# When the q and k of late attention steps are prepared: a reordering between VectorE, ScalarE and the pieces of an MLP

## Chip, core, metric

One core of a Trainium2 chip (trn2). The time is device microseconds of one execution, the median of several. All executions quoted were fast, with a granted TensorE clock of 0.997 to 1.0. A profile is one execution; its span (202.6 us before) is some 1.75 us shorter than its device time (204.35 us in that execution).

Names: PE is TensorE, DVE is VectorE, ACT is ScalarE, POOL is GpSimd, SPq is the queue of DMA issues of SyncE. A "piece" is about 0.87 us of MLP matmuls that the program can place freely; `fill(n)` emits n of them. In the lines of the profile, gT is the gelu output of the first MLP layer, gs the sums of its blocks, MA to MD the PSUM banks of the second layer's products, qkT the transposed q and k, and Hps, S, OK, O and K the banks of the first layer and of attention.

## The reference, cut

```python
# attention in blocks of 64, B=4, H=8, S=768, D=64, with a decay lam per head
intra = (qb @ kb^T) * Dmask ;  out = intra @ vb + (qb * lam_pow) @ kv_state
kv_state = lam**64 * kv_state + (kb * rev_pow)^T @ vb
# then an MLP over x = out as [3072, 512]
g = gelu_tanh(x @ w_in)        # 512 -> 2048
return g @ w_out               # 2048 -> 512
```

## The kernel before

Attention runs in 24 steps (a batch, 256 tokens, half the heads). For each step q, k and v are loaded, prepared (scaled and cast to 16 bits) and q and k transposed; the MLP of finished groups fills PE between the steps. The second MLP layer forms two-by-two block products from sums of blocks (`gs`), so VectorE works for PE before and after each product.

```python
qkp = ctx.enter_context(tc.tile_pool(name="qkp", bufs=4))      # transposed q and k
ps_M = ctx.enter_context(tc.tile_pool(name="psM", bufs=8, space=PSUM))  # all PSUM banks

def prep_qk(s):
    ...
    q_eng = nc.gpsimd if s == 3 else nc.vector
    pin(q_eng.tensor_tensor(wide(tq), q32[:], decay(dq, s), ALU.mult))       # L243
    ...
    pin(nc.scalar.activation(out=wide(tk), in_=k32[:], func=AF.Copy))        # L248
    ...
    if s >= FIRST_DMA_T:                                                     # 9
        pin(nc.sync.dma_start_transpose(out=o..., in_=tqk...))               # L252
# prep_v: v scaled on GpSimd (L230), then the load of step s + 3 is issued

def sum_g(i0, i1, ms=None):        # the sums gs of the second layer, on VectorE
    ...
    pin(nc.vector.tensor_tensor(gsum[m][:, i, :], block(...), block(...), op))   # L531

def product(m, p):                 # one piece: 8 matmuls, banks MA, MB, MC, MD
    ...
    elif m == 6:                   # after the last product of a pair
        pin(tt(d, banks["D"][:], d, ALU.add))                                # L587
```

The order of the late steps, which the change touches:

```python
for n in range(8, 16):
    stage_t(n)
    prep_qk(n + 2) if n == 8 else prep(n + 2)
    fill(3 if n == 14 else 2)
    R(n, n - 1)                    # scores of n, values of n - 1
    ...
for n in range(16, NSTEP + 1, 2):
    if n + 2 < NSTEP:
        prep(n + 2)
    fill(2)
    burst((n, n + 1) if n < NSTEP else (), (15,) if n == 16 else (n - 2, n - 1))
    if n == NSTEP:
        break
    fill(2)
    U(n)
    U(n + 1)
    if n + 3 < NSTEP:
        prep(n + 3)
    fill(14 if n % 4 else 8)
```

`burst` is the attention stretch of two steps: scores S (L295), values O (L379), states K (L393). Every L before belongs to this file.

## Time and profile before

| | before |
|---|---|
| time, 3 runs | 203.91 us (203.87 to 204.37) |
| span of the profile | 202.6 us |
| PE busy | 194.3 us, 96% |
| VectorE busy | 145.4 us, 72% |

PE is the bound: from 17 us to 199 us its matmuls follow each other, but for a few holes. An instruction of PE that starts later than the one before it allows is the thing to look for, not the idle share of other engines.

### The profile page before, as it was taken

To read this page: it belongs to the slowest core of one execution; us is meant where nothing else is said; L and a number is where in the kernel's file an instruction comes from. 1 tells how busy PE (TensorE), PEld (TensorE's weight loads), DVE (VectorE), ACT (ScalarE), POOL (GpSimd) and SP (SyncE) were. 2 spreads that over 40 slices of the span, in tenths; PEclk is the share of its full clock that TensorE was granted. 3 is DMA by queue.
4 is the path that set the end of the run, shared out by engine and by line. 5 is a ranking of instruction groups with operands and counts; after the bars stand their busy time and mean duration, and the time that the engine had idled before them with its cause. 6 is when DMAs were issued, how large, how long until landed. Compare 5 with 4: busy or idle time off the path is not lost.

```text
span 202.6 us, 5666 instructions
## 1 busy us (share of the span) xinstructions
PE 194.3 (96%) x2348; PEld 129.9 (64%) x2348; DVE 145.4 (72%) x293; ACT 107.8 (53%) x205; POOL 66.3 (33%) x80
## 2 busy tenths in 40 slices
PE   6789999999999999999999999999999999999993
PEld 1456544456888888654688764688664688545882
DVE  5896623889999989968799749889556471334753
ACT  2465778375993473487642378524367414466210
POOL 6594132457358254162541609203402000000000
PEclk9999999999999999999999999999999999999999
DMA  6999999999999999999975999305510003300014
GB/s 173 290 328 389 383 387 377 289 292 308 345 256 220 266 207 240 204 271 166 239 193 115 282 230 208 70 0 130 133 58 3 0 0 107 104 0 0 3 45 162
DMA packets 64202, 37.85 MB, mean 187 GB/s; under 512 B 17585, under 2 KB 59569, under 8 KB 64177
## 3 DMA queue, kind: packets, MB, share of 16 engines
q1 hardware_dynamic: 63344, 36.97, 72.1%
q10 hardware_dynamic: 832, 0.52, 0.8%
q8 instruction: 18, 0.29, 0.6%
q14 instruction: 8, 0.06, 0.1%
HBM read 27.26 MB, written 6.29 MB: 166 GB/s over the span
## 4 chain that ended last, share of the span: by engine, by line
PE 77%; DVE 11%; SPq 4%; DMA 4%; issue 2%; ACT 1%; DVEq 0%
PE Hps L484 34%; PE MD L555 7%; PE MB L555 7%; PE O2ps L499 7%; PE MA L555 7%; DVE gs L531 4%; SPq L70 4%; DMA wi<-in_moe_w_in_dram 4%; PE MC L555 3%; PE Hps L601 3%; PE S L295 2%; DVE qk L243 2%; DVE PT L305 2%; PE OK L353 1%; PE Tps L266 1%
## 5 line engine op out<-in xcount | busy, mean ns | idle before, releaser
L484 PE MATMUL Hps<-xT,w_in 128*128 128x512 f16 (+1 forms) x416 | 78.7, 346 | 0.0
L488 ACT ACTIVATE gT<-Hps 128x512 f16<-128x512 f32 x88 | 52.3, 597 | 29.5 <-PE Hps L484 28.5
L484 PEld LDWEIGHTS <-w_in 128*128 128x128 f16 x416 | 40.3, 98 | 33.7
L531 DVE TENSOR_TENSOR gs<-gT 128x1024 f16<-128x1024 f16 (+1 forms) x62 | 39.9, 699 | 18.5 <-ACT gT L488 18.5
L456 POOL TENSOR_TENSOR u<-t,lumask 128x256 f16<-128x256 f32 x40 | 29.4, 747 | 67.8 <-DVE t L449 49.8
L555 PEld LDWEIGHTS <-gs 128*128 128x128 f16 x400 | 38.9, 98 | 5.0 <-DVE gs L531 0.5
L305 DVE TENSOR_TENSOR PT<-S,mask 128x512 f16<-128x512 f32 x48 | 30.4, 681 | 9.5 <-PE S L295 9.5
L230 POOL TENSOR_TENSOR v<-v,dv 128x512 f16<-128x512 f32 x24 | 28.5, 1193 | 4.9 <-PE S L295 1.7
L555 PE MATMUL MA<-w_sum,gT 128*128 128x256 f16 x160 | 19.5, 273 | 0.4 <-DVE o L587 0.3
L555 PE MATMUL MB<-w_out,gs 128*128 128x256 f16 x160 | 19.1, 273 | 0.0
L555 PE MATMUL MD<-w_sum,gs 128*128 128x256 f16 x152 | 18.6, 273 | 0.3 <-DVE gs L531 0.3
L562 ACT ACTIVATE m<-MB 128x512 f32<-128x512 f32 x10 | 6.0, 597 | 23.9 <-PE MB L555 23.9
L248 ACT ACTIVATE qk<-k 128x512 f16<-128x512 f32 x24 | 15.0, 626 | 6.8 <-DMA k<-in_k_dram 6.8
L243 DVE TENSOR_TENSOR qk<-q,dq 128x512 f16<-128x512 f32 x23 | 18.5, 803 | 0.0
L555 PEld LDWEIGHTS <-gT 128*128 128x128 f16 x160 | 15.4, 98 | 3.5 <-ACT gT L488 0.5
L430 ACT ACTIVATE xT<-OK 128x256 f16<-128x256 f32 x29 | 11.2, 455 | 8.0 <-PE OK L353 7.7
L499 PE MATMUL O2ps<-w_out,gT 128*128 128x512 f16 x64 | 14.6, 379 | 0.0
L566 DVE TENSOR_TENSOR o<-MA,m 128x512 f32<-128x512 f32 x10 | 6.9, 688 | 10.2 <-ACT m L562 10.2
L128 DVE TENSOR_TENSOR w_sum<-w_out 128x1024 f16<-128x1024 f16 x10 | 8.9, 932 | 6.4 <-POOL w_out L118 3.5
L430 ACT ACTIVATE xT<-O 128x256 f16<-128x256 f32 x18 | 6.4, 458 | 10.2 <-PE O L404 7.9
L295 PEld LDWEIGHTS <-qkT 64*64 64x64 f16 x384 | 6.0, 106 | 7.0 <-issue 3.2
L449 DVE SCALAR_TENSOR_TENSOR t<-t,lamu,OK 128x64 f32<-128x64 f32 x44 | 10.1, 273 | 0.5
(68 smaller groups left out, 168.7 us busy)
## 6 DMA issues: line engine op xcount, KB each, us to landing
q<-in_q_dram SPq DMA_DIRECT2D x24, 256.0 KB, 5.2
k<-in_k_dram SPq DMA_DIRECT2D x24, 256.0 KB, 5.2
v<-in_v_dram SPq DMA_DIRECT2D x23, 256.0 KB, 5.3
out_dram<-o SPq DMA_DIRECT2D x22, 256.0 KB, 4.5
wo<-in_moe_w_out_dram SPq DMA_DIRECT2D x4, 1024.0 KB, 9.5
wi<-in_moe_w_in_dram SPq DMA_DIRECT2D x4, 512.0 KB, 7.8
wi<-in_moe_w_in_dram SPq DMA_DIRECT2D x2, 1024.0 KB, 12.8
v<-in_v_dram ACTq DMA_DIRECT2D x1, 256.0 KB, 4.3
```

The source lines that it names most:

```text
L230: pin(nc.gpsimd.tensor_tensor(wide(tv[:]), ld32[s][2][:], decay(dv, s), ALU.mult))
L243: pin(q_eng.tensor_tensor(wide(tq), q32[:], decay(dq, s), ALU.mult))
L248: pin(nc.scalar.activation(out=wide(tk), in_=k32[:], func=AF.Copy))
L305: pin(nc.vector.tensor_tensor(t[:, hl].rearrange("p b c d -> p b (c d)"), Sps[:].rearrange("p b c d -> p b (c d)"), mask[:].unsqueeze(1).t ...
L430: pin(nc.scalar.activation(out=d, in_=o, func=AF.Copy))
L449: pin(nc.vector.scalar_tensor_tensor(t[:, hp, :], state[half][:, hp, :], lamu[:, 2 * half + hp : 2 * half + hp + 1], K[:, hp, :], ALU.mult ...
L456: pin(nc.gpsimd.tensor_tensor(u[:], state[half][:].unsqueeze(2).to_broadcast([P, 2, 2, D]), lumask[:, 2 * half : 2 * half + 2, :].unsqueez ...
L484: pin(nc.tensor.matmul(by_block(Hps[:, i, :]), w_in16[:, c, f * P : (f + 1) * P], x(c), start=(c == 0), stop=(c == NC - 1)))
L488: pin(nc.scalar.activation(out=dst, in_=Hps[:], func=AF.Gelu_apprx_tanh))
L499: pin(nc.tensor.matmul(O2[tau][0][:], gT[:, f % HF, f // HF, tau * P : (tau + 1) * P], w_out16[:, f, :], start=(n == 0), stop=(n == NF - 1)))
L531: pin(nc.vector.tensor_tensor(gsum[m][:, i, :], block(T0, F0, i), block(T1, F1, i), op))
L555: pin(nc.tensor.matmul(dst, lhsT, rhs, start=(i == 0), stop=(i == HF - 1), skip_group_check=True))
```

## The change

Intent: have q and k of late steps ready earlier than two pieces ahead of the attention stretch that they are prepared before, and keep the preparation of step 11 from standing in front of the MLP's work.

```diff
     for n in range(8, 16):
         stage_t(n)
+        fill(1 if n == 9 else 0)
         prep_qk(n + 2) if n == 8 else prep(n + 2)
-        fill(3 if n == 14 else 2)
+        fill({9: 1, 14: 3}.get(n, 2))
         R(n, n - 1)
...
-    for n in range(16, NSTEP + 1, 2):
-        if n + 2 < NSTEP:
-            prep(n + 2)
-        fill(2)
-        burst((n, n + 1) if n < NSTEP else (), (15,) if n == 16 else (n - 2, n - 1))
-        if n == NSTEP:
-            break
+    prep(18)
+    fill(2)
+    for n in range(16, NSTEP, 2):
+        burst((n, n + 1), (15,) if n == 16 else (n - 2, n - 1))
         fill(2)
         U(n)
         U(n + 1)
-        if n + 3 < NSTEP:
-            prep(n + 3)
-        fill(14 if n % 4 else 8)
+        for m in (n + 3, n + 4):
+            if m < NSTEP:
+                prep(m)
+            fill(4 if m % 2 == 0 and n % 4 == 0 else 6 if m % 2 == 0 else 6 if n % 4 == 0 else 10)
+    burst((), (NSTEP - 2, NSTEP - 1))
```

PE runs the same matmuls in the same order. Step 11 comes one piece later; step 20 four and step 22 six pieces ahead of the stretch that follows instead of two. That stretch is the one of steps 18 and 19, or of 20 and 21: a step's own scores come one stretch later.

## The prediction

> **What bounds the kernel now.** I read the page first (busy time), then the list of PE's waits, then the timeline around each wait, and last the DMA queue.
>
> Part 1 of the page:
> ```profile
> span 202.6 us, 5666 instructions
> PE 194.3 (96%) x2348; PEld 129.9 (64%) x2348; DVE 145.4 (72%) x293; ACT 107.8 (53%) x205; POOL 66.3 (33%) x80
> ```
> PE fills 96% of the span. A busy PE need not be at its peak, so I also looked at the distance between starts: on the chain, 64 first-layer matmuls of 512 columns take 13.81 us, 216 ns each, and 16 of 256 columns take 1.75 us, 109 ns each. Where the spacing is that, nothing is to be gained. Listing every start that comes later gives, from 20.5 us to the end of PE's work near 199 us, holes of 0.17 us at 39.63, 0.43 at 66.16, 0.22 at 76.03, 0.45 at 108.10, 0.33 at 137.31, and about 0.09 ahead of each of several score stretches: about 2 us, 1% of 203.91. More than that no reordering after the start can win, and the change touches a part of it.
>
> PE's waits between 60 and 142 us (in total, times, longest):
> ```profile
> PE MA L555 <- DVE o L587: 0.3, 1, 0.3
> PE MD L555 <- DVE gs L531: 0.3, 1, 0.3
> ```
> Both are for VectorE: the first is the hole at 108.10, the second that at 66.16. The timeline of 54 to 67 us (start, duration, engine, line, what) around the latter:
> ```profile
> 62.01 2.94 POOL L230 TENSOR_TENSOR v<-v,dv 128x512 f16<-128x512 f32 x2
> ...
> 63.97 1.53 DVE L243 TENSOR_TENSOR qk<-q,dq 128x512 f16<-128x512 f32 x1
> ...
> 64.85 1.04 PE L555 MATMUL MD<-w_sum,gs 128*128 128x256 f16 x8
> 65.42 0.68 DVE L531 TENSOR_TENSOR gs<-gT 128x1024 f16<-128x1024 f16 x1
> ...
> 66.16 1.05 PE L555 MATMUL MD<-w_sum,gs 128*128 128x256 f16 x8 [0.27 <-DVE gs L531]
> ```
> The seventh product would start at 64.85 + 8 x 0.109 = 65.72; it starts at 66.16, because its sum (gs) ends at 66.10, and that stands in VectorE's queue behind step 11's q multiplication (L243).
>
> What comes next on the two engines, 66 to 78 us:
> ```profile
> 69.40 0.45 DVE L449 SCALAR_TENSOR_TENSOR t<-t,lamu,OK 128x64 f32<-128x64 f32 x2
> ...
> 69.78 0.68 DVE L587 TENSOR_TENSOR o<-MD,o 128x512 f32<-128x512 f32 x1
> ...
> 70.11 0.40 PE L344 MATMUL OK<-PT,v 64*64 64x128 f16 x14
> ...
> 70.68 4.53 PE L484 MATMUL Hps<-xT,w_in 128*128 128x256 f16 x40
> ```
> VectorE runs without a gap here (11.26 us busy of 66 to 78). The second L449 ends at 69.85 and frees the PSUM bank that the L344 matmuls first write at 70.06; L587 ends at 70.45 and frees the one that L484 opens at 70.68 (I matched the semaphore values in the built program with their instructions to see which one frees which). A released PE starts 0.05 us after its releaser's end (66.10 to 66.15), so slack is only 0.16 and 0.18 us.
>
> The other place, 113 to 152 us:
> ```profile
> 134.21 1.91 PE L555 MATMUL MD<-w_sum,gs 128*128 128x256 f16 x16
> ...
> 135.38 0.68 DVE L575 TENSOR_TENSOR o<-MC,o 128x512 f32<-128x512 f32 x1
> 135.97 0.68 DVE L243 TENSOR_TENSOR qk<-q,dq 128x512 f16<-128x512 f32 x1
> ...
> 136.57 0.69 DVE L587 TENSOR_TENSOR o<-MD,o 128x512 f32<-128x512 f32 x1
> 136.97 0.19 PE L393 MATMUL K<-v,qk 64*64 64x64 f16 x1
> 137.17 2.48 DVE L305 TENSOR_TENSOR PT<-S,mask 128x512 f16<-128x512 f32 x4
> ...
> 137.31 0.44 PE L393 MATMUL K<-v,qk 64*64 64x64 f16 x31
> ...
> 137.92 1.91 PE L555 MATMUL MA<-w_sum,gT 128*128 128x256 f16 x16
> ```
> One K matmul has run, the other 31 wait for the bank that L587 frees at 137.26. L587 is late because step 22's L243 stands ahead of it. The product at 137.92 in turn follows the first L305 (ends 137.85).
>
> **What the Trainium skill says.** "Perfetto Trace Analysis", section Identifying the Most-Contended Engine, says matmul busy share is no good measure of PE's headroom; this trace agrees (mean duration of L484 346 ns, spacing 216), and that is why I count by starts. Its section Matmuls asks for rotating PSUM banks so that evacuation overlaps the next group; here eight banks rotate, and the hole at 137.31 is where the rotation catches up with VectorE. "GPSIMD Engine Reference", section Key points, says GpSimd shares its SBUF interfaces with VectorE and contends with instructions of two SBUF inputs. The trace agrees: L243 takes 1.53 us beside v on POOL (62.01 to 64.95) and 0.68 us alone; the gs sum at 62.52, also two SBUF inputs, 1.53 too; L305, which reads PSUM, is never stretched. "VectorE: DVE Perf Modes", section on the TRN2 errata, gives (N+151)/0.96 ns for a float32 tensor_tensor: 691 ns at 512; the trace has 680 to 690.
>
> **The change part by part.** The built programs show the same instructions, PE's in the same order; only VectorE, ScalarE and the DMA queue have a few rows exchanged. So no work is removed; the sum is of waits.
>
> 1. Step 11 behind one piece: gs before L243. L243's slot, 63.97, is taken by gs, still beside POOL's v, whose place does not move; I give it the stretched 1.53 us, end 65.50, release 65.55, before the 65.72 at which PE needs it. The 0.43 us at 66.16 go. L243 follows uncontended, so VectorE is free at 66.02 as before.
> 2. Given back at 70: VectorE's own work there is unchanged and gapless, so its banks come free at 69.90 and 70.50 whatever PE does. PE arrives 0.43 earlier but can use 0.16. I book 0.16 us for this part. From there the chain returns to PE (L484, then gT on ScalarE, idle 0.28 before each), so 0.16 travels on.
> 3. Step 20: its q multiplication keeps its place on VectorE; only the k copy on ScalarE moves ahead of gelus, 117.49 to about 115.8. The DMA transpose behind it still starts at 120.37, when the scores' stretch has freed one of the four qkT buffers. Worth 0.
> 4. Step 22, six pieces ahead of its old stretch: L243 goes between gs sums near 131.5. POOL is idle there, so 0.60 us (start spacing of L305, 137.17 to 137.77). The three sums behind it have slack of 1.6 to 2.2 us in my matching, so they bear it. L587 then starts when the products end, 134.21 + 1.91 = 136.12, say 136.16, ends 136.85, and releases at 136.90, before the K matmul needs it (136.98). Saves 0.33. The first L305 moves to 136.76, ends 137.45, releases at 137.50; MA would stand at 137.92 - 0.33 = 137.59. That holds by 0.09. Booked: 0.32.
> 5. Step 23 and steps 19, 21: same order. The holes at 76.03 (a k copy before a gelu) and 108.10 (step 18's L243 before L587) are not touched.
>
> Sum: 0.16 + 0.32 = 0.48; 203.91 - 0.48 = 203.43, about 203.4.
>
> **The rivals.** (a) Nothing is given back at 70: 0.43 + 0.32 = 0.75, 203.15. For it: if gs beside POOL is shorter than 1.53, VectorE runs ahead. Against: the gapless stretch. (b) A transfer decides: prepared four or six pieces ahead, q and k could reach the scores sooner. Against it: no score stretch waits for a transpose. The DMA queue between 105 and 146 us:
> ```profile
> 120.37 1.26 SPq L252 DMA_TRANSPOSE qkT<-qk  x1
> ...
> 124.58 14.70 SPq L252 DMA_TRANSPOSE qkT<-qk  x2
> ```
> The second of that pair, step 22's, stands until the buffer is freed at 138.0, and is needed at 148.44 only. So the early preparation waits in the queue: 0. (c) VectorE is now late elsewhere: gs stretched past 65.72, or step 22's L243 pushing a sum past its product. The slack of 1.6 us speaks against the second; the first would cost part of 0.43, leaving 0.32 alone: 203.6. (d) A new wait of ScalarE or a shift of contention: some tenths, 204.0 to 204.3.
>
> **Range and chances.** The three times of before spread 0.5 us, as wide as the gain, so the range is not narrower: 202.9 (all of (a) and a little luck) to 204.1 (nothing won). A gain of 2% is 4.1 us, twice all holes there are; a loss of 2% would need a chain of new waits, which no slack that I found announces. Faster by over 2%: 0.01; within: 0.98; slower: 0.01.
>
> **What would show it.** The wait of MD for gs gone and gs starting near 64.0 with 1.5 us; a new hole of some 0.27 us at the L344 matmuls; the K matmuls without a hole; L587 there right behind the products; the transposes' starts unmoved; PE's busy time the same within 0.3 us, the span 0.3 to 0.8 shorter. I am wrong if PE's work itself stretches, if a score stretch waits for qkT, or if the hole at 108.10 changes.

## The result, and the profile after

The first comparison: 203.88 us (4 runs, 203.58 to 204.13) against 203.89 us (4 runs, 203.81 to 204.37), ratio 0.9994, interval 0.9973 to 1.0015. A ratio here is the mean time of one kernel's fast runs over that of the other's of the same rounds, so not quite the ratio of the medians. Two further comparisons of the same kernel (below) gave 0.9977 and 0.9968; the mean of the three is 0.998, 0.4 us. Weighted by their intervals they give 0.9983 (0.9968 to 0.9997), an estimate that takes the three as independent and only just leaves out 1. Within 2%, as predicted; whether anything was gained the first comparison could not tell.

The trace can. Part 1 of the page after:
```profile
span 202.2 us, 5666 instructions
PE 194.2 (96%) x2348; PEld 130.1 (64%) x2348; DVE 145.7 (72%) x293; ACT 107.9 (53%) x205; POOL 66.3 (33%) x80
```
PE's waits between 60 and 142 us, after: the one for gs is gone.
```profile
PE MA L555 <- DVE o L587: 0.3, 1, 0.3
```
The timeline of 54 to 67 us, after:
```profile
61.23 4.36 DVE L531 TENSOR_TENSOR gs<-gT 128x512 f16<-128x512 f16 x4
...
62.11 2.94 POOL L230 TENSOR_TENSOR v<-v,dv 128x512 f16<-128x512 f32 x2
...
64.96 1.91 PE L555 MATMUL MD<-w_sum,gs 128*128 128x256 f16 x16
65.52 0.68 DVE L243 TENSOR_TENSOR qk<-q,dq 128x512 f16<-128x512 f32 x1
```
The four sums now stand ahead of L243, and MD is one row of 16 matmuls without a break where there were two rows of 8. The last sum runs from 64.07 to 65.60 in the trace, 1.53 us, and its product starts at 65.83. The sum is loaded as weights, and that load starts at 65.72.

66 to 78 us, after:
```profile
69.50 0.46 DVE L449 SCALAR_TENSOR_TENSOR t<-t,lamu,OK 128x64 f32<-128x64 f32 x2
69.66 0.29 PE L330 MATMUL OK<-v,qk 64*64 64x64 f16 x8
69.79 0.64 PE L344 MATMUL OK<-PT,v 64*64 64x128 f16 x16
69.88 0.68 DVE L587 TENSOR_TENSOR o<-MD,o 128x512 f32<-128x512 f32 x1
...
70.61 4.53 PE L484 MATMUL Hps<-xT,w_in 128*128 128x256 f16 x40
```
VectorE's rows stand 0.10 us later than before, as the whole trace does here (see the table below), so unmoved; PE has come forward to them. The L344 row takes 0.64 us for what takes 0.40 without a wait: it opens on one bank and waits until 70.01 for the one that L449 frees at 69.96. L484 starts 0.05 us after L587's end, 70.56.

113 to 152 us, after:
```profile
131.28 0.69 DVE L243 TENSOR_TENSOR qk<-q,dq 128x512 f16<-128x512 f32 x1
...
134.14 1.91 PE L555 MATMUL MD<-w_sum,gs 128*128 128x256 f16 x16
...
136.09 0.69 DVE L587 TENSOR_TENSOR o<-MD,o 128x512 f32<-128x512 f32 x1
...
136.70 2.47 DVE L305 TENSOR_TENSOR PT<-S,mask 128x512 f16<-128x512 f32 x4
136.90 0.45 PE L393 MATMUL K<-v,qk 64*64 64x64 f16 x32
...
137.51 1.91 PE L555 MATMUL MA<-w_sum,gT 128*128 128x256 f16 x16
```
L587 follows the products directly, the 32 K matmuls are one row, and MA comes 0.41 us earlier on the clock of the trace, 0.33 us of it won here. The DMA queue, 105 to 150 us, after:
```profile
120.30 1.26 SPq L252 DMA_TRANSPOSE qkT<-qk  x1
...
123.65 15.22 SPq L252 DMA_TRANSPOSE qkT<-qk  x2
```
The transposes of steps 20 and 22 start when they did before, apart from the 0.07 and 0.41 us by which the whole trace is ahead there: 120.30 (120.37) and 137.64 (138.05). Step 21's starts 0.93 us earlier (123.65 against 124.58), as a load ahead of it in the queue was issued in 0.57 us instead of 1.55; no stretch shows it.

**Stretch by stretch.** All traces hold the same 2348 matmuls in the same order (but for at most four neighbours in an attention stretch, whose starts cross), so the n-th of one can be held against the n-th of another. The table has the start of five of them, as a difference to the first trace of the kernel before, in us; the middle columns are what a stretch took more or less.

| kernel | reached 64.85 | 64.85 to 70.68 | 99.09 to 109.84 | 136.05 to 139.66 | in all, at 198.40 |
|---|---|---|---|---|---|
| after | +0.10 | -0.17 | 0.00 | -0.33 | -0.41 |
| after, again (e1) | +0.81 | -0.44 | 0.00 | -0.33 | +0.04 |
| after, third (e10) | +0.15 | -0.18 | 0.00 | -0.33 | -0.37 |
| step 11 alone (e2) | +0.84 | -0.17 | 0.00 | 0.00 | +0.66 |
| late steps alone (e3) | +0.53 | 0.00 | 0.00 | -0.33 | +0.20 |
| after, q11 on POOL (e4) | +0.72 | -0.44 | 0.00 | -0.33 | -0.05 |
| before, q22 three times (e5) | 0.00 | 0.00 | 0.00 | +1.45 | +1.44 |
| after, five buffers (e6) | +0.76 | -0.18 | 0.00 | -0.33 | +0.24 |
| after, step 18 later (e7) | +1.49 | -0.19 | -0.41 | -0.33 | +0.56 |
| all together (e8) | +0.12 | -0.44 | -0.41 | -0.33 | -1.06 |
| before itself (e9) | +0.58 | -0.01 | 0.00 | 0.00 | +0.56 |
| all together, again (e11) | +0.17 | -0.44 | -0.41 | -0.33 | -1.01 |

The stretches that are not shown differ by 0.01 us or less. So the change wins 0.50 us where it was made, and the first 65 us, in which PE has the same work in the same order in all of these kernels, scatter by up to 1.49 us and hide it. Most of that is there after 20 us: the matmul at 20.45 us in the first trace stands between -0.05 and +1.40 us in the others.

### The profile page after: what moved, and what is told of

Its sections match the earlier page's. It is cut to its first block, busy times and chain, and to the rows that moved or that the text cites. A ratio compares the mean times of both kernels' runs of the same rounds, so it can differ in the third digit from the quotient of the medians.

```text
span 202.2 us, 5666 instructions
## 1 busy us (share of the span) xinstructions
PE 194.2 (96%) x2348; PEld 130.1 (64%) x2348; DVE 145.7 (72%) x293; ACT 107.9 (53%) x205; POOL 66.3 (33%) x80
## 4 chain that ended last, share of the span: by engine, by line
PE 81%; DVE 6%; SPq 4%; DMA 4%; ACT 2%; issue 2%; DVEq 0%
PE Hps L484 37%; PE MB L555 8%; PE MA L555 8%; PE MD L555 7%; SPq L70 4%; PE MC L555 4%; DMA wi<-in_moe_w_in_dram 4%; PE Hps L601 3%; PE O2ps L499 3%; PE S L295 3%; DVE w_sum L128 2%; PE OK L353 2%; PE OK L344 1%; PE Tps L266 1%; DVE gs L531 1%
## 5 line engine op out<-in xcount | busy, mean ns | idle before, releaser
L484 PE MATMUL Hps<-xT,w_in 128*128 128x512 f16 (+1 forms) x416 | 78.7, 346 | 0.0
L484 PEld LDWEIGHTS <-w_in 128*128 128x128 f16 x416 | 40.4, 98 | 33.7
L531 DVE TENSOR_TENSOR gs<-gT 128x1024 f16<-128x1024 f16 (+1 forms) x62 | 40.8, 712 | 18.3 <-ACT gT L488 18.3
L305 DVE TENSOR_TENSOR PT<-S,mask 128x512 f16<-128x512 f32 x48 | 30.4, 682 | 9.5 <-PE S L295 9.5
L243 DVE TENSOR_TENSOR qk<-q,dq 128x512 f16<-128x512 f32 x23 | 17.6, 767 | 0.0
L449 DVE SCALAR_TENSOR_TENSOR t<-t,lamu,OK 128x64 f32<-128x64 f32 x44 | 10.1, 273 | 0.5
```

Of the source, the lines that this page charges most:

```text
L305: pin(nc.vector.tensor_tensor(t[:, hl].rearrange("p b c d -> p b (c d)"), Sps[:].rearrange("p b c d -> p b (c d)"), mask[:].unsqueeze(1).t ...
L484: pin(nc.tensor.matmul(by_block(Hps[:, i, :]), w_in16[:, c, f * P : (f + 1) * P], x(c), start=(c == 0), stop=(c == NC - 1)))
L531: pin(nc.vector.tensor_tensor(gsum[m][:, i, :], block(T0, F0, i), block(T1, F1, i), op))
```

## The experiments

Four kernels at a time shared a chip and the runs of the kernel before, three in the last call.

**e1, the changed kernel again.** No edit.

> The changed kernel again, in five rounds, to narrow the interval of the first comparison (0.9973 to 1.0015). My theory (a gain of 0.48 us, from which the first comparison's noise hid most): ratio 0.9976, 203.4 where the kernel before gives 203.9, and in the profile the distance from the score product near 60 us to the one near 187 us shorter by 0.50 us. The rival that the change is worth nothing: ratio 1.000 with an interval that leaves out 0.998.

Measured: 204.12 us against 204.38, ratio 0.9977 (0.9950 to 1.0004). The interval leaves out neither theory by itself, though the middle is where mine put it. The trace gained more around 66 us than expected, 0.44 instead of 0.17. In this execution ScalarE waited 2.7 us for a store of the output near 50 us, PE waited for ScalarE's gT near 54 and 61 us, and came to the stretch 0.81 us late; from 60 to 71 us:
```profile
61.84 2.67 DVE L531 TENSOR_TENSOR gs<-gT 128x512 f16<-128x512 f16 x4
...
64.44 0.68 DVE L243 TENSOR_TENSOR qk<-q,dq 128x512 f16<-128x512 f32 x1
...
64.66 2.36 POOL L230 TENSOR_TENSOR v<-v,dv 128x512 f16<-128x512 f32 x2 [1.90 <-PE OK L344]
```
The four sums took 2.67 us, not 4.36: POOL's v had to wait for PE and came only after them. VectorE was then so far ahead that nothing was given back. Lateness alone does not do it: e2 came 0.84 us late, with the usual collision, and gave back as usual. That v's delay is the reason is read from this one trace, and no run tests it.

**e2, step 11 alone.**
```diff
 # the kernel before, with this part of the change only
+        fill(1 if n == 9 else 0)
         prep_qk(n + 2) if n == 8 else prep(n + 2)
-        fill(3 if n == 14 else 2)
+        fill({9: 1, 14: 3}.get(n, 2))
```

> Only the part that puts step 11's q and k behind one piece of the MLP. By my sum it is worth 0.16 us (ratio 0.9992): the product MD starts 0.43 us earlier, and a hole of some 0.25 us opens near 70 us, at the L344 matmuls, with L587's end 0.05 us ahead of the L484 after it. If nothing were given back, 0.43 us and no hole at 70 us. The hole near 137 us (0.33 us) stays.

Measured: ratio 1.0006 (0.9975 to 1.0038), which tells nothing at this size. The trace: 0.17 us won, MD unbroken, the long L344 row there (0.64 us), and the hole at 137 us as before.

**e3, the late steps alone.** The rest of the diff, without the two lines of e2.

> Only the late part (steps 20, 22 and 23 moved, step 11 as before). By my sum 0.32 us (ratio 0.9984): the hole near 137 us gone, that at 66 us (0.43 us) as in the kernel before, no hole at 70 us. If the late part were worth nothing because the transposes wait in the queue anyway: 1.000 and the hole at 137 us still there or moved to the next bank.

Measured: ratio 0.9976 (0.9947 to 1.0005); trace: nothing at 66 us, 0.33 us at 137 us. The two parts add up: 0.17 + 0.33 = 0.50.

**e4, step 11's q on GpSimd.**
```diff
 # the changed kernel
-        q_eng = nc.gpsimd if s == 3 else nc.vector
+        q_eng = nc.gpsimd if s in (3, 11) else nc.vector
```

> The changed kernel with step 11's q multiplication on GpSimd instead of VectorE. If VectorE's backlog is what takes back the gain at 70 us, all its work after the gs sum comes 0.6 us earlier, the hole at the L344 matmuls is gone, and the stretch is 0.27 us shorter than in the changed kernel: 0.75 us under the kernel before, ratio 0.9963. If something else held PE at 70 us (a transfer, ScalarE), the hole stays and the time is that of the changed kernel, 0.9976.

Measured: ratio 0.9977 (0.9949 to 1.0004). The stretch is 0.44 us shorter than before, 0.27 shorter than in the first trace of the changed kernel, and the L344 row is the short one of 0.40 us (63 to 72 us):
```profile
69.52 0.46 DVE L449 SCALAR_TENSOR_TENSOR t<-t,lamu,OK 128x64 f32<-128x64 f32 x2
...
70.40 0.40 PE L344 MATMUL OK<-PT,v 64*64 64x128 f16 x14
```
The second L449 is now done well ahead of the matmuls that need its bank. So it was VectorE's backlog that took back 0.27 us, and 0.6 us less of it is enough. In the time it cannot be told from e1, whose trace gained the same 0.44 us by chance.

**e5, step 22's q three times.**
```diff
 # the kernel before
-        pin(q_eng.tensor_tensor(wide(tq), q32[:], decay(dq, s), ALU.mult))
+        for _ in range(3 if s == 22 else 1):
+            pin(q_eng.tensor_tensor(wide(tq), q32[:], decay(dq, s), ALU.mult))
```

> The kernel before with step 22's q multiplication written three times (same values), so 1.20 us more on VectorE just ahead of L587 in the stretch near 137 us. If the K matmuls wait for L587, and L587 for what stands before it, the hole there grows from 0.33 to about 1.5 us and the stretch from 136 to 140 us is 1.2 us longer (ratio 1.006). If that hole belongs to something else (the transpose, ScalarE's evacuation), nothing or far less than 1.2 us comes.

Measured: 205.94 us against 204.17, ratio 1.0084 (1.0064 to 1.0104). 134 to 140.5 us (lines are one higher here):
```profile
135.97 2.13 DVE L244 TENSOR_TENSOR qk<-q,dq 128x512 f16<-128x512 f32 x3
...
138.02 0.68 DVE L588 TENSOR_TENSOR o<-MD,o 128x512 f32<-128x512 f32 x1
...
138.75 0.44 PE L394 MATMUL K<-v,qk 64*64 64x64 f16 x31 [1.60 <-DVE o L588]
```
L588, which is L587 elsewhere, starts 1.45 us later, and the stretch is 1.45 us longer: what was put ahead of it on VectorE is added on PE. That it is 1.45 and not 1.20 comes from the starts of the three, 0.71 and 0.73 us apart instead of 0.60: the built program makes each wait for VectorE's own semaphore, since they write the same tile. Mechanism shown, and in the time too.

**e6, five qkT buffers.** Six did not fit in SBUF. So five, with a t buffer fewer.
```diff
 # the changed kernel
-    qkp = ctx.enter_context(tc.tile_pool(name="qkp", bufs=4))
+    qkp = ctx.enter_context(tc.tile_pool(name="qkp", bufs=5))
-    ucp = ctx.enter_context(tc.tile_pool(name="ucp", bufs=3))
+    ucp = ctx.enter_context(tc.tile_pool(name="ucp", bufs=2))
```

> The changed kernel with five qkT buffers instead of four (and two t buffers instead of three, to make room). Step 22's transpose then needs the buffer that is freed near 120 us, and should start near 132 us instead of 137.7, step 20's near 117 instead of 120.3. By my reading no score stretch waits for them, so the time is that of the changed kernel (every stretch after 70 us within 0.1 us). If the rival is right that an earlier transpose is where the gain lies, the stretches with scores near 136 and 148 us get shorter.

Measured: ratio 1.0013 (0.9987 to 1.0039). The DMA queue, 105 to 150 us:
```profile
124.29 9.71 SPq L252 DMA_TRANSPOSE qkT<-qk  x2
```
and 132 to 150 us, where the second of these stands alone:
```profile
132.76 1.24 SPq L252 DMA_TRANSPOSE qkT<-qk  x1
```
This one, step 22's, starts at 132.76 instead of 137.64; step 20's only at 119.45, because two output stores stand ahead of it. No stretch changed by more than 0.02 us against the changed kernel. An earlier transpose is worth nothing here: the rival falls. (The interval of the time leaves out the 0.9976 that was expected; see e8 on the times.)

**e7, step 18 after the products.**
```diff
 # the changed kernel
-    prep(18)
     fill(2)
+    prep(18)
```

> The changed kernel with step 18's q and k prepared after the two pieces ahead of the stretch near 106 us, not before them, so that L587 stands ahead of L243 on VectorE. The same reasoning as for step 22: L587 starts 0.6 us earlier, the hole of 0.45 us at the product near 108 us is gone, 0.45 us under the changed kernel, ratio about 0.9955. If the product waits for something else there, the hole stays. L243 and the transpose come 0.6 us later, which should cost nothing, as the scores of step 18 stand 10 us behind.

Measured: ratio 0.9988 (0.9960 to 1.0016), with the latest arrival of all at 65 us (+1.49); the expected 0.9955 lies just outside this interval. Before, from 94 to 113 us:
```profile
106.76 0.69 DVE L243 TENSOR_TENSOR qk<-q,dq 128x512 f16<-128x512 f32 x1
...
107.36 0.69 DVE L587 TENSOR_TENSOR o<-MD,o 128x512 f32<-128x512 f32 x1
...
108.10 1.91 PE L555 MATMUL MA<-w_sum,gT 128*128 128x256 f16 x16 [0.34 <-DVE o L587]
```
In e7, 105 to 112 us:
```profile
108.25 0.69 DVE L587 TENSOR_TENSOR o<-MD,o 128x512 f32<-128x512 f32 x1
...
108.86 0.68 DVE L243 TENSOR_TENSOR qk<-q,dq 128x512 f16<-128x512 f32 x1
...
108.99 1.91 PE L555 MATMUL MA<-w_sum,gT 128*128 128x256 f16 x16
```
The order is turned round, and the stretch is 0.41 us shorter; the 0.04 that is missing is the rest of the same wait (L587 ends at 108.94, MA starts 0.05 later). The reasoning on step 22 holds for a place that the change left alone.

**e8 and e11, all together.** The edits of e4 and e7 on the changed kernel.

> The changed kernel with step 11's q on GpSimd and step 18 after the products. If the parts add up: 0.43 + 0.45 + 0.33 = 1.21 us less than the kernel before in the stretches after 60 us, ratio about 0.994, about 202.8 us where the kernel before gives 204.0. If they give each other's gain back, less than 1 us.

> The version with all three parts again. The stretches of its first trace give 1.18 us (ratio 0.994), the first timing gave 0.9967 (0.67 us). If the difference was the scatter of the early stretches, this one lies nearer 0.994, and the mean of both between; if it is real, again near 0.9967.

Measured: 203.33 us against 204.17, ratio 0.9967 (0.9949 to 0.9985), and 203.59 against 204.74, ratio 0.9952 (0.9921 to 0.9984). Both traces have the three parts, 0.44 + 0.41 + 0.33 = 1.18 us, to the hundredth, and the list of PE's waits between 60 and 142 us is empty in the first (the hole of 0.22 us at 76.03, which that list does not show, is still there, now at 75.71). This version is faster than the kernel before, by 0.3 to 0.5%: both intervals leave out 1. With the changed kernel it was set side by side, 203.59 against 203.98 us (ratios 0.9952 and 0.9968, intervals that overlap), so that it beats that one too is shown by the traces (0.68 us less in the stretches) and not yet by the time. The mean of the two ratios, 0.9960, is 0.82 us; the trace's 1.18 us would be 0.9942, which lies in the second interval and just outside the first. What the difference is stays open. A likely part: all four ratios of e5 to e8 lie above what their stretches give (1.0084 against 1.0071, 1.0013 against 0.9975, 0.9988 against 0.9954, 0.9967 against 0.9942). They share one set of runs of the kernel before, with a mean of 204.25 us where the other two had 204.49 and 204.68; a set that happened to be quick raises all four alike. No run tests this.

**e9, the kernel before against itself.** No edit.

> The kernel before against itself, to see what the comparison makes of nothing and how far the early stretches scatter. If the scatter of some 0.3% comes from the time before 66 us (loads landing), the ratio is 1.000 within about 0.003, the stretches up to 66 us differ from the first trace of the kernel before by up to 1 us, and every stretch after 70 us agrees within 0.02 us. If the scatter were in the stretches that the change touches, they would differ here too.

Measured: ratio 1.0006 (0.9975 to 1.0038). Its trace comes 0.58 us late to 64.85 and agrees within 0.01 us in each stretch after that. So the scatter is the start's, most of it before 20 us: it was 0.31 us late at 15.6 us and 0.76 at 20 us. In this execution, PE stood 0.65 us near 17 us waiting for nothing that the profile shows; in the first trace it waited there for the cast of a weight load that had landed late.

**e10, the changed kernel a third time.** No edit.

> The changed kernel a third time, beside the kernel before itself. Ratio 0.9976 if the 0.50 us that the trace shows come out in the time, 1.000 if they are made good before 66 us; in the trace 0.16 to 0.44 us less in the stretch around 66 us and 0.33 us less around 137 us.

Measured: 203.98 us against 204.74, ratio 0.9968 (0.9939 to 0.9998), the first of the three intervals that leaves out 1. Trace: 0.18 and 0.33 us.

## Why the prediction was right

- **The bound and the ceiling.** PE bounds the kernel, and about 2 us of holes was all that could be won. PE's busy time changed by 0.1 us, and after the first 65 us the two places in question are the only ones where the time changed. Two slips of the reading, without consequence: the 346 ns of L484 are a mean of two shapes, 379 ns with 512 columns and 273 with 256, so that 379 is what stands against the spacing of 216; and VectorE runs "without a gap" only up to 75.27 us, where it waits 0.74 us, which is what 11.26 busy of 12 leaves; the place in question lies before that.
- **Step 1, the sum ahead of L243.** The estimate of 1.53 us beside POOL's v was measured as 1.53 (64.07 to 65.60). The wait is gone. The margin was thinner than the 0.17 us of the working (65.55 to 65.72): that counts to the start of the matmul, but the sum is loaded as weights 0.11 us before it. Released at 65.65 and wanted at 65.72, it was in time by 0.07 us.
- **Step 2, given back at 70.** Booked 0.16, measured 0.17, 0.18, 0.17, 0.18 and 0.19 in five traces, 0.44 in one where POOL's v was late. The hole was foretold as some 0.27 us in one place; it was 0.24 at L344 (0.64 against 0.40) and a few hundredths at L330 and L484. e4 shows the cause.
- **Step 3, step 20 and the transposes.** Booked 0. The k copy moved to 115.70 as foretold; the transpose did not move; e6 shows that moving it is worth nothing.
- **Step 4, step 22.** Booked 0.32, measured 0.33 in all nine traces that have it. L587 was foretold for 136.16 and came at 136.09, in a trace that is 0.07 us ahead there; e5 shows that the wait follows L587.
- **The sum.** 0.48 booked, 0.50 in the trace. The stated time of 203.4 lies 0.5 us under the first median, 203.88, and inside the range. The sum was of stretches after 60 us; the time has the start in it, which in these traces reached 64.85 anywhere from 0.00 to 1.49 us late. The prediction took the spread of three runs (0.5 us) for the scatter; the 33 runs of the kernel before in the three later calls lie between 203.83 and 205.59, which is 1.76 us.
- **What is luck in it.** The range, 202.9 to 204.1, holds the kernel before as well (203.91), so a change worth nothing would have fallen into it too. That the first median lies inside says little; the steps are borne out by the traces.
- **Rivals.** (a) came true in e1 only, with the sums beside no v, as its condition said; (b) fell with e6; (c) and (d) did not show.

## What to carry to other kernels

An engine that keeps pace with the bound on average still stops it where an unneeded instruction stands ahead of a needed one in its queue; so look at what is ahead of the instruction that frees a bank, and put work with microseconds of slack behind it. A gain on the bound counts only up to the next place where the helper's backlog frees a buffer: work out that place's slack before booking the gain. Differences of a few tenths of a microsecond are read from the same instructions in two traces, stretch by stretch; the whole time has the scatter of the start in it.

## What the Trainium skill lacked or had wrong

- "GPSIMD Engine Reference", section Key points, names the contention but gives it no size. "SBUF — State Buffer", section Who interferes with whom, calls it an exclusive lock and mentions slowdowns of 6.8 and 1.5 times without saying of which instructions. The runs agree that they collide: beside POOL's v a VectorE instruction with two SBUF inputs took 1.53 us instead of 0.68, and v 1.49 instead of 1.04; L305, with one input in PSUM, kept 0.68. Neither page says that whether the two collide can change from one execution to the next (four sums in 4.36 us in one, 2.67 in another).
- "VectorE: DVE Perf Modes", section The DRAIN you can't avoid, reports that a semaphore after each of eight copies costs nothing. It has no figure for an instruction that waits for VectorE's own semaphore: starts 0.71 and 0.73 us apart instead of 0.60 (e5).
- "Perfetto Trace Analysis", section "Per-instruction lifecycle: what the profiler-reported window actually captures", shows the propagation of a semaphore without a number. From the end of a VectorE or ScalarE instruction to the start of the PE instruction that it holds, the traces have 0.05 us.
- I found no page that says how far executions of one kernel scatter: up to 1.49 us within the first 65 us here, under 0.02 us in the stretches after 71 us whose order of work is the same.
